# Bounds in one piece, an accumulating form, split constants and measured durations in a two-part attention kernel

## The chip, the cores and the metric

The kernel runs on one core of one Trainium2 chip, as one program. The metric is the device time of one execution in microseconds (us); the time of a kernel is the median of its runs. The engines are TensorE (PE in the profile; its weight loads are listed apart as PEld), VectorE (DVE), ScalarE (ACT), GpSimd (POOL) and SyncE (SP), which here only issues DMAs. TensorE and the others meet in PSUM, eight banks that TensorE writes; all other tiles lie in SBUF.

## What is computed

Two attention blocks over 2048 rows of 1024 columns (32 heads of 32), each with its own input and weights; the outputs stand side by side. Block A is local attention in 4 segments of 512 with a running memory; block B is linear attention with a learned feature map. Cut to what matters:

```python
# A, for each segment s of 4, all heads
logits = einsum("bhqd,bhkd->bhqk", qs, ks) * scale + mask      # causal inside the segment
a_dot  = softmax(logits) @ vs
a_mem  = (phi(qs) @ M) / (phi(qs) @ z + 1e-6)                  # phi(t) = t + 1 if t > 0 else exp(t)
o      = g * a_mem + (1 - g) * a_dot                           # g = sigmoid(beta), one per head
M += phi(ks)^T @ vs;  z += sum(phi(ks))
out_a  = o @ wo
# B
pq, pk = q @ w_phi, k @ w_phi                                  # per head, 32 x 32
phi_x  = concat(softmax(px), softmax(-px))
o      = (phi_q @ (phi_k^T @ v)) / (phi_q @ sum(phi_k) + 1e-6)
out_b  = o @ B_wo
```

## The kernel before

**Numbers.** All large products are made from float16 halves. A float32 operand is scaled, split into a high and a low half, and each product is three matmuls (high-high, high-low, low-high) into one PSUM bank. For that every operand needs a scale, and every result a bound from which its own scale follows. The helper `halves` makes the two halves (ACT the high one, line 427; DVE the low one, line 429), `halved` loads a piece, takes its largest sums of absolute values (ACT, line 469, or DVE, line 463) and calls `scale` (a tiny matmul, line 411, and two DVE instructions, lines 413 and 415) and then `halves`.

**Stages.** The first stage, up to about 900 us, does block A's attention in 32 units (`units`): a unit is one segment of 512 rows and one group of four heads. The first 16 units take segments 0 and 1, the last 16 segments 2 and 3, so each of the eight weight groups is used in both halves; group numbers 8 to 15 stand for the second use. For a unit, `produce` multiplies the q and k weights with the segment (line 400), scales the result by the unit's bounds and moves it into the layout for the scores; `values` does the same for v; `attend` does the attention. The second stage does block B in eight pairs of row tiles (`expo`, the key sums at line 1345, then the queries and their output `project`), with products in Strassen's form of seven products per 2 x 2 blocks (line 596). The last stage is block A's output projection in the same form (line 1590).

**The bounds.** `bounds(k, segs, prio)` works out, for weight group k and one or two segments, the bounds of q and k and what follows from them, in a small tile `bd`: one fp32 matmul per segment (line 708) gives the products of the segment's and the weights' sizes; DVE and POOL make a scale, its reciprocal and five more rows from it (lines 711 to 724). `bounds_v` (lines 733 to 744) does so for v, in `bv`, and keeps the running largest bound in `big` (line 740). In the second half `bounds` is called once for each of groups 8 to 15 and `bounds_v` once for each of the v weights 4 to 7, at the units that load those weights.

**The maxima.** Inside `attend`, `maxima` makes the scores of a block of rows in PSUM (line 854), and DVE adds the causal mask and takes each row's largest (line 860) into `mt`, a 128 x 4 x 4 tile. Two small DVE instructions split `mt` into a high and a low float16 half, `mh` (lines 874 and 875). TensorE turns these into rows (line 880), ACT copies them into the unit's q tile `stk` (line 882), and a DMA repeats them for the other heads. The scores proper (line 945) then carry the subtraction of the largest in the product itself: rows 96 to 103 of the k side hold constants.

**The opening.** Those constants are written once, by three ACT instructions over 8 x 2048 elements (line 637), one for each of the three `stk` tiles; the source `sel` is made by DVE just before (lines 346 to 349). The first transfers are the first weights and the first segment (line 447). The halves of the first groups' weights are made by POOL and ACT (lines 421, 423 and 424): POOL scales the piece, ACT copies the high half, POOL subtracts it; for the first segment and the first v weights `halves` uses ACT and DVE.

**The order.** The engines' queues are in order, and the order is not that of the code. Each `op(engine, duration, function, reads, writes, prio)` is kept in a list; `Graph.run` at the end plays the program through in its own time, and issues the instructions in the order in which that play starts them: at each step the engine that can start earliest takes, of the operations that could start then, the one with the lowest priority number. The durations written in the calls are what this play goes by. A DMA there takes 0.6 us to issue, a fixed latency and its KB over 230 per us. `port=True` (and every POOL operation) means that DVE and POOL operations of this kind don't run side by side in the play. A priority is the number in the call plus a `nudge`: the operations are counted in blocks of 60, and for blocks that stand in `NUDGE` each operation's priority is shifted by a fixed pseudo-random amount, up to 0.3, 0.7, 1.5 or 3.0 by the seed's last two bits. In the play's gaps on TensorE `fill` issues matmuls whose result is unused (line 358).

## Time and profile before

| | |
|---|---|
| median of 3 runs | 1703.16 us (1702.68 to 1703.31) |
| the profiled execution | 1704.9 us |
| its span, from the first to the last instruction | 1702.8 us |
| mean granted TensorE clock | 0.994 |
| busy: PE / DVE / ACT / POOL | 1669.9 / 1399.3 / 1113.4 / 1072.7 us |
| DMA | 280.94 MB |

How to read it: the profile is one execution on the chip. Busy times count instructions of an engine; the rest of the span is idle time, and a row of the timeline or of a group names in brackets, or after a bar, the idle time in front of it and the engine and line that ended it. The granted clock is the share of TensorE's full clock: at 0.5 a matmul takes twice as long, and TensorE counts as busy all the while. Lines are those of the kernel before.

### The profile page before, as it was taken

What the parts mean: (1) busy time and instruction counts of PE and PEld (TensorE: products, weight loads), DVE (VectorE), ACT (ScalarE), POOL (GpSimd) and SP (SyncE); (2) the same over time, 40 slices, a digit from 0 to 9 for tenths busy, and PEclk for the clock granted to TensorE, in tenths of its full rate; (3) what the DMA queues carried; (4) which work ended last, traced back from release to release, by engine and by line L of the source; (5) the groups of instructions that cost most, each with busy time, mean ns of one, the idle gap of its engine ahead of it and who ended that gap; (6) DMA issues with size and microseconds to landing.
All of it is one profiled execution on the core that took longest, in us unless ns stands there. A gap on an engine that the chain in (4) does not pass through costs nothing.

```text
span 1702.8 us, 38814 instructions
## 1 busy us (share of the span) xinstructions
PE 1669.9 (98%) x14520; PEld 1001.0 (59%) x14520; DVE 1399.3 (82%) x3225; ACT 1113.4 (65%) x2027; POOL 1072.7 (63%) x1431
## 2 busy tenths in 40 slices
PE   8999999999999999999999999999999999999999
PEld 6766767676676667766754444444544444444444
DVE  7999999988898788787897998987997777886441
ACT  7779789876786687676776757754765554444331
POOL 6757777676786887867766544454689898541000
PEclk9999999999999999999999999999999999999999
DMA  6964676747656554657567335346566675565311
GB/s 218 236 178 101 155 184 188 222 130 207 167 146 168 131 148 123 158 183 192 138 206 285 119 118 179 131 173 247 207 161 149 174 186 137 171 176 167 117 64 62
DMA packets 266044, 280.94 MB, mean 165 GB/s; under 512 B 162816, under 2 KB 215808, under 8 KB 257280
## 3 DMA queue, kind: packets, MB, share of 16 engines
q1 hardware_dynamic: 265856, 278.47, 56.4%
q8 instruction: 114, 1.87, 0.5%
q14 instruction: 74, 0.61, 0.1%
HBM read 144.39 MB, written 85.00 MB: 135 GB/s over the span
## 4 chain that ended last, share of the span: by engine, by line
PE 59%; DVE 13%; ACT 3%; issue 1%; DMA 1%; POOL 1%; SPq 0%; ACTq 0%; DVEq 0%; POOLq 0%
PE proj L400 14%; PE proj L596 11%; PE misc L400 10%; PE proj L1590 5%; PE s L1590 2%; PE s L945 2%; PE s L854 2%; PE pv L981 2%; DVE mx L1191 2%; PE s L596 2%; DVE r L1201 1%; PE pv L1526 1%; DVE S L429 1%; PE misc L1590 1%; PE misc L596 1%
## 5 line engine op out<-in xcount | busy, mean ns | idle before, releaser
L400 PE MATMUL proj<-S,S 128*128 128x128 f16 (+1 forms) x3072 | 503.3, 300 | 2.1 <-ACT S L427 0.7
L400 PEld LDWEIGHTS <-S 128*128 128x128 f16 x4608 | 331.2, 99 | 150.3 <-issue 4.0
L596 PE MATMUL proj<-S,S 128*128 128x512 f16 x1488 | 348.4, 381 | 6.7 <-DVE cs L606 2.4
L596 PEld LDWEIGHTS <-S 128*128 128x128 f16 x1968 | 187.5, 98 | 220.3 <-issue 9.6
L958 POOL TENSOR_SCALAR_AFFINE_SELECT ph<-ph 128x256 f16<-128x256 f16 (+1 forms) x448 | 193.2, 453 | 131.1 <-DVE ph L952 103.2
L860 DVE CUSTOM_DVE_ANT_0 s<-s,causal 128x256 f32<-128x256 f32 (+3 forms) x512 | 241.9, 511 | 13.3 <-PE s L854 10.4
L952 DVE SCALAR_TENSOR_TENSOR ph<-s,ph 128x512 f16<-128x512 f32 x320 | 210.4, 684 | 41.6 <-ACT ph L951 38.5
L949 ACT ACTIVATE s<-s,bd 128x512 f32<-128x512 f32 x320 | 211.0, 706 | 47.7 <-PE s L945 46.6
L951 ACT ACTIVATE ph<-s 128x512 f16<-128x512 f32 x320 | 186.8, 647 | 6.3 <-PE pv L981 2.6
L400 PE MATMUL misc<-S,ot 128*128 128x512 f16 x768 | 170.5, 379 | 0.1
L1198 ACT ACTIVATE e<-e,sk 128x256 f32<-128x256 f32 x256 | 114.5, 500 | 71.5 <-DVE e L1195 67.6
L400 PEld LDWEIGHTS <-ot 128*128 128x128 f16 x768 | 73.7, 98 | 88.1
L945 PE MATMUL s<-S 104*128 104x512 f16 (+3 forms) x512 | 114.4, 300 | 0.7 <-DVE ph L952 0.3
L854 PE MATMUL s<-S 96*128 96x512 f16 (+3 forms) x512 | 112.0, 299 | 2.7 <-DVE ph L952 2.5
L1495 POOL TENSOR_TENSOR e<-e,zb 128x512 f32<-128x512 f32 x64 | 85.4, 1348 | 33.8 <-DVE r L1201 33.1
L400 PE MATMUL proj<-wv,S 128*128 128x128 f16 x1536 | 105.1, 219 | 0.0
L981 PEld LDWEIGHTS <-ph 128*128 128x128 f16 x2560 | 87.4, 96 | 18.6 <-issue 1.3
L981 PE MATMUL pv<-vl,ph 128*128 128x66 f16 (+1 forms) x2560 | 92.7, 184 | 1.5 <-DVE mt L860 0.5
L1201 DVE TENSOR_REDUCE r<-e 128x32 f32<-128x1024 f32 x64 | 77.0, 1209 | 14.8 <-ACT e L1198 14.8
L1338 POOL TENSOR_TENSOR pt<-e,pt 128x512 f16<-128x512 f32 x40 | 50.1, 1264 | 49.2 <-ACT pt L1335 49.2
L596 PE MATMUL s<-S,S 128*128 128x512 f16 x324 | 77.6, 379 | 0.0
L860 DVE DVE_READ_ACCUMULATOR2_ANT mt<- 128x1 f32 x512 | 72.8, 142 | 0.0
(334 smaller groups left out, 3317.0 us busy)
## 6 DMA issues: line engine op xcount, KB each, us to landing
S<-h SPq DMA_DIRECT2D x192, 128.0 KB
S<-wf_d SPq DMA_DIRECT2D x21, 1024.0 KB
st<-bwqk SPq DMA_DIRECT2D x64, 256.0 KB
wf_d<-fo SPq DMA_DIRECT2D x48, 256.0 KB
out<-os SPq DMA_DIRECT2D x39, 256.0 KB
wf_d<-oT SPq DMA_DIRECT2D x36, 256.0 KB
S<-xf_d SPq DMA_DIRECT2D x9, 1024.0 KB
S<-aw SPq DMA_DIRECT2D x16, 512.0 KB
```

Source lines behind the costliest of these rows:

```text
L400: op(PE, dur, lambda c=c, a=a, b=b, lv=lv, rv=rv: nc.tensor.matmul(pv(), lv(), rv(), start=(c == 0 and a + b == 0), stop=(c == n - 1 and a ...
L596: op(PE, 0.215, lambda n=n, a=a, b=b, lv=lv, rv=rv: nc.tensor.matmul(ps(), lv(), rv(), start=(start and n == 0 and a + b == 0), stop=(n == ...
L854: nc.tensor.matmul(ps()[:, o:o + 128 * i + 128], st()[0:96, 0, h, 128 * i:128 * i + 128], st()[0:96, 1, h, 0:128 * i + 128], start=True, s ...
L860: dve(0.12 + 0.00113 * n, lambda h=h, i=i, o=o, n=n: nc.vector.tensor_tensor_reduce(ps()[:, o:o + n], ps()[:, o:o + n], causal[:, 512 - n: ...
L945: nc.tensor.matmul(ps()[:, o:o + n], st()[0:104, 1, h, 128 * j:128 * j + 128], st()[0:104, 0, h, 128 * j:512], start=True, stop=True)
L949: act(0.59, lambda: nc.scalar.activation(ps(), ps(), AF.Exp, bias=0.0, scale=bd()[:, 4, i2, 0:1]), r=[(bd, i2)], w=[ps])
L951: act(0.5, lambda: nc.scalar.activation(ph()[:, 0], ps(), AF.Copy, scale=2.0 ** 14), r=[ps], w=[(ph, 0)])
L952: dve(0.6, lambda: nc.vector.scalar_tensor_tensor(ph()[:, 1], ps(), 2.0 ** 14, ph()[:, 0], op0=OP.mult, op1=OP.subtract), r=[ps, (ph, 0)], ...
L958: nc.gpsimd.affine_select(pd, pd, pattern=[[0, n], [1, 128]], compare_op=OP.is_ge, fill=0.0, base=0, channel_multiplier=-1)
L981: nc.tensor.matmul(ps()[:, i, n0:n1], ph()[:, a, o:o + 128], vl()[:, j, h, n0:n1], start=(i == 0 and a == 0), stop=(j == min(i, 2)), skip_ ...
L1198: op(ACT, 0.41, lambda i=i: nc.scalar.activation(e()[:, 4 * i:4 * i + 4], e()[:, 4 * i:4 * i + 4], AF.Exp, bias=0.0, scale=sk()[:, i:i + 1 ...
L1590: op(PE, 0.215, lambda n=n, a=a, b=b: nc.tensor.matmul(ps(), v(a)[:, n, :], wform[w]()[:, b, n, :], start=(start and n == 0 and a + b == 0 ...
```

## The change

1. **Bounds of the second half.** A new function `bounds_late` is called once, at unit 12, for all eight q and k weight groups, all four v weights and both segments. It has four matmuls, nine DVE instructions and eight POOL ones, and needs two PSUM banks. `Part` gives each group its view of the common tiles. The calls of `bounds` and `bounds_v` for the second half go.
2. **Inside `bounds`.** Two of the DVE instructions (lines 714 and 721) read the PSUM bank in place of the row that DVE has just made from it. The second follows the first at once.
3. **The maxima's rows.** The first of the two instructions on `mt` (line 874) also writes a sum, as an accumulator output, into a new fifth row of `mt` that nothing reads.
4. **The opening.** Each of the three writes over 8 x 2048 elements becomes four over 8 x 512, in four separately tracked parts. The call of `load_wg` for the first q weights names DVE in place of POOL, so their halves are made by lines 427 and 429 and not by lines 421, 423 and 424.
5. **The plan.** Some hundred durations in the calls are set to other numbers, five operations are marked as port users, and `NUDGE` has 145 seeds in place of 40. None of these adds or removes an instruction; they change the order in which the instructions are issued.

```diff
-NUDGE = {0: 465887, 3: 912202, 5: 876263, 7: 730503, 8: 455190, 9: 72936, 13: 804475, 14: 476942, 15: 772345, 18: 258321,
...
+NUDGE = {0: 927028, 3: 115959, 4: 583906, 7: 632749, 8: 844680, 9: 362793, 10: 459728, 12: 438123, 14: 268131, 15: 522000,
...
+class Part:
+    def __init__(self, of, at):
+        self.of, self.at = of, at
+
+    def __call__(self):
+        return self.at(self.of())
...
-        op(DVE, 0.1, lambda: nc.vector.tensor_tensor(big[:, 1:2], big[:, 1:2], pst[:, p, 0:1], op=OP.max),
-           r=[(pstb, (p, 0))], w=[(bigs, 1)], prio=prio)
+        op(DVE, 0.13, lambda: nc.vector.tensor_tensor(big[:, 1:2], big[:, 1:2], pst[:, p, 0:1], op=OP.max),
+           r=[(pstb, (p, 0))], w=[(bigs, 1)], prio=prio, port=True)
...
     for t in stk:
-        op(ACT, 2.0, lambda t=t: nc.scalar.activation(t()[96:104, 1], sel[96:104, :, None].to_broadcast([8, 4, 512]), AF.Copy),
-           w=[(t, (1, 3))], prio=0.3)
+        for h in range(4):
+            op(ACT, 0.5, lambda t=t, h=h: nc.scalar.activation(t()[96:104, 1, h], sel[96:104, h:h + 1].to_broadcast([8, 512]), AF.Copy),
+               w=[(t, (1, 3, h))], prio=0.3)
...
         op(DVE, 0.1, lambda: nc.vector.scalar_tensor_tensor(
-            bd()[:, 4, v, 0], bd()[:, 3, v, 0], SCALE, bd()[:, 3, v, 1], op0=OP.mult, op1=OP.mult), w=w, prio=prio)
+            bd()[:, 4, v, 0], ps()[:, v, 0], SCALE * 2.0 ** -12, bd()[:, 3, v, 1], op0=OP.mult, op1=OP.mult), r=[ps], w=w, prio=prio)
+        op(DVE, 0.1, lambda: nc.vector.tensor_scalar(
+            bd()[:, 5, v, 0], ps()[:, v, 1], 2.0 ** -14, 2.0 ** -14, op0=OP.mult, op1=OP.add), r=[ps], w=w, prio=prio)
...
-        op(DVE, 0.1, lambda: nc.vector.tensor_scalar(
-            bd()[:, 5, v, 0], bd()[:, 3, v, 1], 0.25, 2.0 ** -14, op0=OP.mult, op1=OP.add), w=w, prio=prio)
...
+    def bounds_late(prio):
+
+        bd, bv = (G.buf("a", [128, r, n], F32, t) for r, n, t in ((7, 4 * NG, "bdl"), (4, 8, "bvl")))
...
+        ps, pv = bank("misc", [128, 2, NG, 2], "bounds"), bank("misc", [128, 2, 4], "bounds")
+        w, wv = [(bd, 0), (bd, 1)], [(bv, 0), (bv, 1)]
+        for x in range(2):
+            op(PE, 0.14, lambda x=x: nc.tensor.matmul(
+                ps()[:, x].rearrange("p k m -> p (k m)"), xam[:, 2 + x:3 + x].to_broadcast([128, 128]),
+                wgb.rearrange("p k m -> p (k m)"), start=True, stop=True),
+               r=[(xams, 2 + x), *((wgbs, (k, m)) for k in range(NG) for m in range(2))], w=[ps], prio=prio)
...
+        op(DVE, 0.11, lambda: nc.vector.tensor_scalar(b(3), f(ps()), 2.0 ** -12, 1e-30, op0=OP.mult, op1=OP.max), r=[ps], w=w, prio=prio)
...
+        op(DVE, 0.1, lambda: nc.vector.tensor_tensor(big[:, 0:1], big[:, 0:1], c(0)[:, 0:1], op=OP.max), r=wv, w=[(bigs, 0)],
+           prio=prio, port=True)
...
-                op(POOL, 1.57, lambda p=p: nc.gpsimd.tensor_scalar(
+                op(POOL, 1.98, lambda p=p: nc.gpsimd.tensor_scalar(
                     p(), p(), 1.0, bd()[:, 5, i2, 1:2], op0=OP.min, op1=OP.mult), r=[(bd, i2)], w=[p], prio=E)
...
-        mt = G.buf("a", [128, 4, 4], F32, "mt", 2)
+        mt = G.buf("a", [128, 5, 4], F32, "mt", 2)
...
-        dve(0.1, lambda: nc.vector.tensor_scalar(mh()[:, :, 0, :], mv(mt), -(2.0 ** -14), None, op0=OP.mult), r=[mt], w=[(mh, 0)])
+        dve(0.18, lambda: nc.vector.tensor_scalar(
+            mh()[:, :, 0, :], mv(mt), -(2.0 ** -14), None, op0=OP.mult, op1=OP.add, accum_out=mt()[:, 4, 0:1]),
+            r=[mt], w=[(mh, 0), (mt, "sum")])
...
-    load_wg(0, -3, POOL, 10, ms=(0,), after=[(xt[0][0], (0, 3))])
+    load_wg(0, -3, DVE, 10, ms=(0,), after=[(xt[0][0], (0, 3))])
...
+        if u == 12:
+            bounds_late(2 * u + 3.5)
...
-            x = 2 * ((u // 4 + 1) // 4)
-            bounds_v(u // 4 + 1, [x, x + 1], 2 * u + 0.5)
+            if u // 4 + 1 < 4:
+                bounds_v(u // 4 + 1, [0, 1], 2 * u + 0.5)
...
-            x = 2 * ((k + 2) // NG)
-            bounds(k + 2, [x, x + 1], 2 * u + 3.5)
+            if k + 2 < NG:
+                bounds(k + 2, [0, 1], 2 * u + 3.5)
```

## The prediction

> **What bounds the kernel now.** First the page's busy times, then the cores, then the busy times by stretches of 50 us (columns: stretch, its length, busy PE, PE weight loads, DVE, ACT and POOL with their counts, granted clock, DMA share, GB/s).

> ```profile
> span 1702.8 us, 38814 instructions
> PE 1669.9 (98%) x14520; PEld 1001.0 (59%) x14520; DVE 1399.3 (82%) x3225; ACT 1113.4 (65%) x2027; POOL 1072.7 (63%) x1431
> ```

> ```profile
> core 0: 1702.8 us, clock 0.994
> ```

> ```profile
> 0.00:50.00 50.00, 44.88 (x321) 32.47 (x322) 38.09 (x118) 35.27 (x54) 35.02 (x52) 0.97 0.68 229
> 50.00:100.00 50.00, 50.00 (x527) 35.93 (x525) 47.44 (x126) 38.96 (x72) 34.75 (x58) 1.00 0.87 227
> ...
> 350.00:400.00 50.00, 47.28 (x512) 33.21 (x510) 41.31 (x114) 34.87 (x64) 38.46 (x68) 0.97 0.65 180
> 550.00:600.00 50.00, 47.47 (x547) 34.05 (x546) 40.84 (x108) 34.39 (x63) 44.22 (x58) 0.97 0.51 134
> 850.00:900.00 50.00, 46.63 (x371) 27.14 (x370) 45.06 (x123) 38.81 (x69) 33.65 (x45) 0.97 0.61 197
> ...
> 1650.00:1702.80 52.80, 48.91 (x227) 21.98 (x225) 9.99 (x14) 10.49 (x16) 0.00 (x0) 1.00 0.16 60
> ```

> TensorE is the bound: busy 1669.9 of 1702.8 us, 50.00 of 50 in an ordinary stretch. So TensorE work that goes is worth its full length, and work taken off another engine is worth only the TensorE stop that it ends. There are 1702.8 - 1669.9 = 32.9 us of stops, and the clock of 0.994 loses another 0.006 x 1702.8 = 10.2 us. The stops are not spread evenly: the opening has 5.1 us, the end 3.9 us, and a few stretches have about 3 us each, with the clock at 0.97 there (0.03 x 50 = 1.5 us lost). I looked into such stretches for what stood in front of TensorE.

> **Part 1: the bounds of the second half.** Today `bounds` (line 708) and `bounds_v` (line 733) each issue two small fp32 matmuls per call, and each matmul leaves two records.

> ```profile
> 364.13 0.50 PE L708 MATMUL misc<-wgb,xam 128*128 128x2 f32 x4
> ...
> 364.49 0.58 PE L733 MATMUL misc<-wvb,xam 128*128 128x1 f32 x4
> ...
> 364.94 0.38 PE L945 MATMUL s<-S 104*128 104x512 f16 x1
> ```

> ```profile
> L708 PE MATMUL misc<-wgb,xam 128*128 128x2 f32 x64 | 9.4, 242 | 0.2 <-DVE ph L952 0.2
> ...
> L733 PE MATMUL misc<-wvb,xam 128*128 128x1 f32 x32 | 4.6, 244 | 0.0
> ```

> These eight records hold TensorE from 364.13 to 364.94, which is 0.81 us or 0.10 us each. Half of all records belong to the second half (32 of line 708, 16 of line 733). The new `bounds_late` has four matmuls, eight records: 48 - 8 = 40 records go, 40 x 0.10 = **-4.0 us**, on TensorE itself. The bounds of this term are -4.0 and 0 (0 where TensorE would stop for something else). 52 small DVE instructions and 40 of POOL also go, and 9 and 8 come (counted in the code). I cost that at nothing: TensorE covers it. Should the cover fail, the new run of nine DVE instructions at 0.15 to 0.2 us delays what is queued behind it, the attention of units 12 and 13, by under 2 us once. The same holds for the two misc banks that `bounds_late` keeps until its last reader.

> **Part 2: two stops at which DVE waited for POOL.** The timeline around 561 us (start, length, engine, line, in brackets the idle time before it and who ended it):

> ```profile
> 560.59 1.13 POOL L958 TENSOR_SCALAR_AFFINE_SELECT ph<-ph 128x256 f16<-128x256 f16 x3
> ...
> 560.97 4.13 DVE L874 TENSOR_SCALAR mh<-mt 128x16 f16<-128x16 f32 x1
> ...
> 561.69 1.15 POOL L507 TENSOR_TENSOR fo<-quad,fo 128x512 f16<-128x512 f32 x1
> ...
> 562.81 1.15 POOL L507 TENSOR_TENSOR oT<-quad,oT 128x512 f16<-128x512 f32 x1
> ...
> 563.92 1.15 POOL L809 TENSOR_TENSOR pkh<-pk,pkh 128x512 f16<-128x512 f32 x1
> ...
> 565.90 0.39 PE L880 MATMUL misc<-identr,mh 128*8 128x128 f16 x4 [2.53 <-DVE mh L875]
> ```

> ```profile
> L874 DVE TENSOR_SCALAR mh<-mt x32: 158/196/4133, 51.1 to 882.4; 128x16 f16<-128x16 f32 x32
> ```

> ```profile
> L874 DVE TENSOR_SCALAR mh<-mt 128x16 f16<-128x16 f32 x32 | 14.3, 447 | 0.2
> ```

> ```profile
> L875 DVE SCALAR_TENSOR_TENSOR mh<-mh,mt x32: 106/178/1243, 53.3 to 882.6; 128x16 f16<-128x16 f16 x32
> ```

> The rows give each line's shortest, median and longest in ns, and for line 874 also the total in us and the mean. A DVE instruction over 16 elements, median 196 ns, mean 447, takes 4.13 us, exactly while POOL runs without a pause (from 560.59 to 565.07), and TensorE stops 2.53 us for its result. Line 875, which reads two SBUF tensors, takes at most 1.24 us. The same kind of thing, twice in a row, at 366 us:

> ```profile
> 366.38 1.04 DVE L714 SCALAR_TENSOR_TENSOR bd<-bd 128x2 f32<-128x2 f32 x1
> ...
> 367.33 1.19 DVE L740 SCALAR_TENSOR_TENSOR big<-bv,big 128x1 f32<-128x1 f32 x1
> ...
> 369.18 0.58 PE L854 MATMUL s<-S 96*128 96x384 f16 x2 [2.09 <-DVE ph L952]
> ```

> Each stop has a tail in which the granted clock drops (stretches of 7.5 us, the clock is the third number from the end):

> ```profile
> 365.00:372.50 7.50, 4.78 (x37) 3.61 (x37) 7.50 (x18) 7.50 (x15) 7.27 (x11) 0.78 0.47 94
> 565.00:572.50 7.50, 6.60 (x28) 2.85 (x29) 3.24 (x9) 3.61 (x7) 3.31 (x5) 0.77 0.58 127
> ```

> Lost to the clock: 7.5 x 0.22 = 1.7 us after the first, 7.5 x 0.23 = 1.7 us after the second. So the stop at 561 costs 2.53 + 1.7 = 4.2 us and the one at 366 costs 2.09 + 1.7 = 3.8 us. The change rewrites all three instructions. Line 874 gets an accumulator output, lines 714 and 721 read PSUM in place of SBUF, and the second half's calls of line 740 shrink to one. I take both stops as gone: **-4.2 and -3.8 us** (bounds: all of it, or nothing). What is late next at 561 us is the vl low half (line 767), which is queued behind line 874 anyway.

> [...]

> The accumulator adds a read per call, which the trace shows for line 860:

> ```profile
> L860 DVE DVE_READ_ACCUMULATOR2_ANT mt<- 128x1 f32 x512 | 72.8, 142 | 0.0
> ```

> That is 32 x 0.142 = 4.5 us more DVE, against 32 x (447 - 196) ns, 8 us, of waits that go. The read is taken at that row's length; it could be nothing if it hides in the instruction. DVE has 2.6 us free even from 50 to 100, and 4.5 us over the 831 us between the first and the last call are 0.27 per 50: nothing. Without that cover each read would delay line 880 by 0.14 us.

> **Part 3: the opening.**

> ```profile
> 4.25 3.70 ACT L637 ACTIVATE S<-sel 8x2048 f16<-8x2048 f32 x2 [2.19 <-DVE sel L349]
> ...
> 7.98 1.06 ACT L469 ACTIVATE S<-S 128x1024 f16<-128x1024 f32 x1
> ...
> 9.60 0.16 DVE L413 TENSOR_SCALAR wgs<-misc 128x1 f32<-128x1 f32 x1 [2.57 <-PE misc L411]
> ...
> 22.17 3.10 POOL L421 TENSOR_SCALAR S<-S,wgs 128x512 f32<-128x512 f32 x2 [6.21 <-issue]
> ...
> 24.31 1.32 ACT L427 ACTIVATE wv<-S,wvs 128x512 f16<-128x512 f32 x2
> ...
> 25.24 3.14 POOL L424 TENSOR_TENSOR S<-S,S 128x512 f16<-128x512 f32 x2
> ...
> 27.88 1.72 DVE L429 SCALAR_TENSOR_TENSOR wv<-S,wvs,wv 128x512 f16<-128x512 f32 x2
> ...
> 28.44 1.46 PE L400 MATMUL proj<-S,S 128*128 128x512 f16 x6
> ```

> *The constants.* ACT writes two constants before it sizes the first weights (line 469), and DVE stands 2.57 us in front of line 413 for that size, with the maxima of the first segment queued behind. Pieces of a quarter would let line 469 in sooner, but the order is fixed by the plan. In the plan the weights' transfer is ready at 0.6 + 1.0 + 512 / 230 + 0.1 = 3.9 us and ACT starts at 0, so two pieces of 2.0 go ahead of line 469 now and eight of 0.5 will. On the chip ACT starts at 4.25. Eight pieces take between 8 x 0.46 = 3.7 us (a quarter of 1.85) and 8 x 0.66 = 5.3 us (line 427, equally long); 0.6 each is nearer to the second row, since a shorter instruction keeps its fixed part. That is 4.8 in place of 3.7: **+1.1 us**. Bounds: -2.6 us, the whole wait of line 413, if fewer pieces go ahead, and +1.6.
> *The first q weights.* Their halves are made by POOL, ACT and POOL (lines 421, 423, 424) from 22.17 to 25.24 + 3.14 = 28.38, and TensorE's q product goes on at 28.44. The call now names DVE, so ACT and DVE make them (lines 427 and 429): 0.66 + 2 x 0.86 = 2.4 us by the rows in place of 6.2, **-3.8 us**, since TensorE has little else there. Bounds: -3.8, and +1.7 if the two DVE instructions only push back the low halves of the v weights, which end at 27.88 + 1.72 = 29.60 and are due next on TensorE. POOL's 6.2 us go too; the halves of the next group's weights are next there.

> **Part 4: the new costs and seeds of the plan** add no work; they re-draw the order of the whole kernel. Left after part 2 are 32.9 - 5.1 - 3.9 - 2.5 - 2.1 = 19.3 us of stops and 10.2 - 1.5 - 3.4 = 5.3 us of clock: at most -24.6 us. Upwards it can add stops such as those of part 2, at 4.0 us each; I allow five, +20. One of the stretches that remain shows instructions whose plan entry becomes a port user:

> ```profile
> 882.65 1.10 DVE L875 SCALAR_TENSOR_TENSOR mh<-mh,mt 128x16 f16<-128x16 f16 x1
> ...
> 883.75 1.09 DVE L551 TENSOR_TENSOR big<-big,pst 128x1 f32<-128x1 f32 x1
> ...
> 883.80 0.22 PE L880 MATMUL misc<-identr,mh 128*8 128x128 f16 x1 [0.91 <-DVE mh L875]
> ```

> Line 551 is now planned as a port user, with 0.13 us. I take that one stretch as mended (850 to 900: 3.37 us of stops and 1.5 of clock, **-4.9 us**) and the others as drawn again with the same loss. This is the softest term.

> **The sum**: -4.0 - 4.2 - 3.8 + 1.1 - 3.8 - 4.9 = -19.6 us. The profiled execution took 1704.9 us with its span of 1702.8, so it would take 1685.3; the median of the runs, 1703.16, lies 1.7 below it, so the forecast is **1683.6 us**.

> **Rivals.**
> *The redrawn order stops TensorE more often (slower).* From 50 to 100 DVE is busy 47.4 of 50, so a late DVE instruction reaches TensorE; each new stop with its half clock costs 4.0 us. Parts 1 to 3 give -14.7, so it decides from five more stops than remain: 1703.2 - 14.7 + 5 x 4.0 = 1708.5 us. For it: everything is redrawn. Against it: 4.2 + 3.8 us of stops came from instructions that no longer meet POOL. Chance 0.17.
> *The wait only moves.* Line 875 follows at once and still reads two SBUF tensors; if it inherits the 4.13 us, part 2 gives 3.8 only and the time is 1687.8 us. Against it: its longest is 1.24 us in 32. Chance 0.08.
> *The time is given back.* If the matmuls, the two stops and the earlier q weights all turn into waits on DVE, and the order mends nothing, the time stays at 1703.2 us. For it: DVE's 47.4 of 50 early on. Against it: 41 of 50 where these stops lie. Chance 0.07.

> **How the numbers follow.** The forecast, with the order between its best and an even draw, has the remaining 0.68. A measurement of this kernel tells about 0.2% from no change, 3.4 us. Faster takes the forecast and the moved wait, 0.76; same 0.07; slower 0.17. The range goes from 1703.2 - 14.7 - 24.6 = 1663.9, about 1664, up to the slower rival at about 1709.

> **What would show it.** Right: line 874 never over 0.6 us; 48 records on lines 708 and 733 of the first half plus 8 new ones; no half clock after a DVE wait on POOL near the unit 12 bounds; line 469 starting near 9 us; the first q product done before 30 us. Wrong: more than five half clocks after the opening, line 875 over 2 us, or PE stops of over 33 us in total.

## The result, and the profile after

| | before | after |
|---|---|---|
| median | 1703.24 us (1702.68 to 1704.99, 4 runs) | 1675.91 us (1673.94 to 1676.12, 4 runs) |
| ratio | | 0.9835, 95% interval 0.9818 to 0.9852 |
| profiled span | 1702.8 us | 1673.8 us |
| TensorE stops (span less busy) | 32.9 us | 26.2 us |
| lost to the granted clock | 0.006 x 1702.8 = 10.2 us | 0.001 x 1673.8 = 1.7 us |
| filler matmuls, records | 64 | 18 |

The losses to the clock come from a mean clock given to three places, so they are good to about 0.9 us. The change takes off 27.3 us; the forecast was 19.6. From here on lines are those of the kernel after, unless another kernel is named; before's lines 400, 469, 714, 740, 874 and 875 are now 420, 489, 735, 761, 952 and 955.

First the page's busy times and the clock of the kernel after:

```profile
span 1673.8 us, 38587 instructions
...
PE 1647.6 (98%) x14434; PEld 984.4 (59%) x14434; DVE 1374.2 (82%) x3216; ACT 1106.0 (66%) x2036; POOL 1066.1 (64%) x1395
```

```profile
core 0: 1673.8 us, clock 0.999
```

TensorE is still the bound. It has 86 records fewer (14520 less 14434): the 40 of the bounds and 46 of the filler. Now the busy times by stretches, for those in which before had lost most:

```profile
0.00:50.00 50.00, 43.90 (x332) 30.73 (x333) 38.76 (x127) 38.15 (x67) 30.22 (x51) 1.00 0.77 251
...
350.00:400.00 50.00, 49.71 (x530) 35.68 (x528) 46.49 (x147) 32.49 (x58) 37.01 (x57) 1.00 0.84 204
550.00:600.00 50.00, 50.00 (x561) 35.24 (x558) 41.94 (x131) 41.59 (x79) 39.27 (x61) 1.00 0.54 155
850.00:900.00 50.00, 49.17 (x388) 26.01 (x386) 38.23 (x74) 36.78 (x66) 36.12 (x52) 1.00 0.69 224
```

The three late stretches, with 2.5 to 3.4 us of stops each and a clock of 0.97 before, have 0.3, 0.0 and 0.8 us of stops and a clock of 1.00. In the whole trace there is no half clock between 5.8 and 1671.5 us. Next the two instructions on `mt`, all 32 calls of each (shortest, median, longest in ns):

```profile
L952 DVE TENSOR_SCALAR_CACHE_REDUCE mh<-mt x32: 164/172/183, 48.0 to 861.1; 128x16 f16<-128x16 f32 x32
L952 DVE DVE_READ_ACCUMULATOR mh<-mt x32: 75/82/89, 48.1 to 861.2; 128x1 f32 x32
```

```profile
L955 DVE SCALAR_TENSOR_TENSOR mh<-mh,mt x32: 169/182/1132, 52.5 to 861.4; 128x16 f16<-128x16 f16 x32
```

The 4133 ns call is gone, the read costs 82 ns, and line 955 did not inherit a long wait here. The filler (its count stands in the row behind the tile) fell from 64 records to 18. First before, then after:

```profile
L358 PE MATMUL fill<-ident x64: 270/275/523, 13.9 to 1424.3; 128*128 128x128 f32 x64
```

```profile
L378 PE MATMUL fill<-ident x18: 270/275/356, 14.4 to 1176.9; 128*128 128x128 f32 x18
```

The spans differ by 29.0 us. Of these 10.2 - 1.7 = 8.5 are clock, 32.9 - 26.2 = 6.7 are stops, 4.1 the bounds' records (the time from the start of each such record to the next, added up in both traces) and about 46 x 0.12 = 5.5 the filler's (0.12 us by the row of equal matmuls quoted in the experiment on the constants). That is 24.8; the other 4.2 are busy time of TensorE that I did not assign.

### The profile page after: what moved, and what is told of

Its sections match the earlier page's. It is cut to its first block, busy times and chain, and to the rows that moved or that the text cites. A ratio compares the mean times of both kernels' runs of the same rounds, so it can differ in the third digit from the quotient of the medians.

```text
span 1673.8 us, 38587 instructions
## 1 busy us (share of the span) xinstructions
PE 1647.6 (98%) x14434; PEld 984.4 (59%) x14434; DVE 1374.2 (82%) x3216; ACT 1106.0 (66%) x2036; POOL 1066.1 (64%) x1395
## 3 DMA queue, kind: packets, MB, share of 16 engines
q8 instruction: 113, 1.85, 0.5%
## 4 chain that ended last, share of the span: by engine, by line
PE 36%; DVE 10%; POOL 7%; ACT 3%; issue 2%; DMA 0%; ACTq 0%; DVEq 0%; POOLq 0%
PE proj L616 10%; PE misc L420 6%; PE proj L1672 5%; PE proj L420 4%; PE s L1672 2%; PE s L616 2%; PE misc L616 1%; POOL e L1577 1%; PE misc L1672 1%; DVE r L1283 1%; DVE mx L1273 1%; POOL e L1589 1%; DVE S L449 1%; PE pv L1608 1%; ACT e L1280 1%
## 5 line engine op out<-in xcount | busy, mean ns | idle before, releaser
L420 PEld LDWEIGHTS <-S 128*128 128x128 f16 x4608 | 326.6, 98 | 143.6 <-POOL S L444 0.7
L616 PE MATMUL proj<-S,S 128*128 128x512 f16 x1488 | 344.9, 379 | 6.6 <-ACT cs L622 4.3
L616 PEld LDWEIGHTS <-S 128*128 128x128 f16 x1968 | 186.8, 98 | 221.7 <-issue 11.7
L938 DVE CUSTOM_DVE_ANT_0 s<-s,causal 128x512 f32<-128x512 f32 (+3 forms) x512 | 241.2, 509 | 12.6 <-PE s L932 10.1
L1031 ACT ACTIVATE ph<-s 128x512 f16<-128x512 f32 x320 | 190.7, 660 | 1.1
L1029 ACT ACTIVATE s<-s,bd 128x512 f32<-128x512 f32 x160 | 107.1, 713 | 16.7 <-PE s L1025 16.3
L1029 ACT ACTIVATE s<-s,bdl 128x512 f32<-128x512 f32 x160 | 105.8, 707 | 6.3 <-PE s L1025 6.1
L1286 POOL TENSOR_SCALAR r<-r 128x32 f32<-128x32 f32 x32 | 12.5, 396 | 96.9 <-DVE r L1284 79.5
```

What stands on the lines that cost most here:

```text
L420: op(PE, dur, lambda c=c, a=a, b=b, lv=lv, rv=rv: nc.tensor.matmul(pv(), lv(), rv(), start=(c == 0 and a + b == 0), stop=(c == n - 1 and a ...
L616: op(PE, 0.2165, lambda n=n, a=a, b=b, lv=lv, rv=rv: nc.tensor.matmul(ps(), lv(), rv(), start=(start and n == 0 and a + b == 0), stop=(n = ...
L938: dve({128: 0.216, 256: 0.381, 384: 0.6, 512: 0.648}[n], lambda h=h, i=i, o=o, n=n: nc.vector.tensor_tensor_reduce(ps()[:, o:o + n], ps()[ ...
L1029: act(0.571, lambda: nc.scalar.activation(ps(), ps(), AF.Exp, bias=0.0, scale=bd()[:, 4, i2, 0:1]), r=[(bd, i2)], w=[ps])
L1031: act(0.478, lambda: nc.scalar.activation(ph()[:, 0], ps(), AF.Copy, scale=2.0 ** 14), r=[ps], w=[(ph, 0)])
```

## The experiments

In all but the four with other seeds, the plan was left as it was: the operations, their durations and their number stay, and only what one of them issues is changed. So, but for the records that an edit adds or moves, TensorE runs the same records in the same order, and the same record can be looked up in two traces. "TensorE stands 1.4 us ahead at 33 us" means that the record which after starts at 33 us starts 1.4 us earlier, each counted from its trace's start. Small leads say little: the next two kernels have before's opening, and yet stand 0.5 and 0.6 us behind it at 33 us.

### The accumulating form alone, in the old order and taken out of the new one

In before, line 874:
```diff
-nc.vector.tensor_scalar(mh()[:, :, 0, :], mv(mt), -(2.0 ** -14), None, op0=OP.mult)
+nc.vector.tensor_scalar(mh()[:, :, 0, :], mv(mt), -(2.0 ** -14), None, op0=OP.mult, op1=OP.add, accum_out=mt()[:, 4, 0:1])
```

> The kernel before, order unchanged, with the accumulating form alone (line 874). Theory: all 32 calls of line 874 take under 0.3 us, the 4.13 us one among them goes, and the time falls by 4.2 us (2.5 us of TensorE's stop and 1.7 us of the half clock behind it), to about 1699.0. Rival, the wait moves to line 875 behind it: that line shows a call of 3 us or more at 561 us, and the time stays within 0.7 us of before.

Measured: 1701.88 us against 1703.63, ratio 0.9989 (0.9980 to 0.9998), so -1.8 us (-0.3 to -3.4). The timeline of this kernel around 561 us:

```profile
561.72 0.17 DVE L874 TENSOR_SCALAR_CACHE_REDUCE mh<-mt 128x16 f16<-128x16 f32 x1
...
562.79 3.05 DVE L875 SCALAR_TENSOR_TENSOR mh<-mh,mt 128x16 f16<-128x16 f16 x1
...
563.54 1.15 POOL L507 TENSOR_TENSOR oT<-quad,oT 128x512 f16<-128x512 f32 x1
...
564.65 1.15 POOL L809 TENSOR_TENSOR pkh<-pk,pkh 128x512 f16<-128x512 f32 x1
...
565.89 0.39 PE L880 MATMUL misc<-identr,mh 128*8 128x128 f16 x4 [1.77 <-DVE mh L875]
```

The rival was right about the mechanism: line 874 takes 0.17 us and line 875, which reads two SBUF tensors, takes the wait, 3.05 us, to the end of the same POOL run. TensorE's stop shrinks from 2.53 to 1.77 us. In the trace TensorE gains 2.4 us at this place, but the kernel of the next experiment, which leaves line 874 alone, gains 1.7 us at the same place: a half clock that did not come. So the form's own part is about 0.8 us, by which the stop shrank. The time came out as neither side had it: less than the theory's 4.2 us, and more than the rival's 0.7.

In after, the other way round (the arguments `op1` and `accum_out` of line 952 taken out):

> The kernel after, order unchanged, with the negated maxima (line 952, 32 calls) in the plain form again. Theory: in the order after too, the plain form must wait for POOL where the accumulating one doesn't: several of the 32 calls take over 0.5 us (accumulating: 164 to 183 ns each), and one or more behind a run of POOL instructions takes 1.6 us or more, so the time rises by 1 to 5 us. Rival, the form alone is worth little and the new order removed the stop: no call takes over 1.6 us, and the time stays within 1 us of after.

Measured: 1676.89 us (1676.43 to 1678.45) against 1675.91 of after; the ratios to before are 0.9846 (0.9833 to 0.9860) and 0.9835 (0.9818 to 0.9852), and the intervals overlap.

```profile
L952 DVE TENSOR_SCALAR mh<-mt x32: 162/312/1459, 48.0 to 862.2; 128x16 f16<-128x16 f32 x32
```

The waits are back (median 312 ns instead of 172, longest 1459), but none is over 1.6 us, and TensorE ends 0.6 us later in the trace. The rival holds: in the new order the form is worth about 1 us, which can't be told from nothing.

### The bounds read from PSUM, in the old order

```diff
-op(DVE, 0.1, lambda: nc.vector.tensor_scalar(bd()[:, 3, v], ps()[:, v], ...), r=[ps], w=w, prio=prio)
+def first():
+    nc.vector.tensor_scalar(bd()[:, 3, v], ps()[:, v], 2.0 ** -12, 1e-30, op0=OP.mult, op1=OP.max)
+    nc.vector.scalar_tensor_tensor(bd()[:, 4, v, 0], ps()[:, v, 0], SCALE * 2.0 ** -12, bd()[:, 3, v, 1], op0=OP.mult, op1=OP.mult)
+    nc.vector.tensor_scalar(bd()[:, 5, v, 0], ps()[:, v, 1], 2.0 ** -14, 2.0 ** -14, op0=OP.mult, op1=OP.add)
+op(DVE, 0.1, first, r=[ps], w=w, prio=prio)
```
The operations of lines 714 and 721 issue nothing.

> The kernel before, order unchanged, with the two products of the bounds (lines 714 and 721) reading PSUM and issued straight behind line 711; line 740 stays as it is. Theory: the stop at 366 us loses the part that lines 714 and 721 make, and the half clock behind it where the rest of the stop is short enough: the time falls by 1.0 to 3.8 us. Rival, line 740 takes the whole wait: it shows a call as long as the three lines' waits together, and the time stays within 0.7 us of before.

Measured: 1704.12 us against 1703.63, ratio 1.0003 (0.9994 to 1.0012): nothing. The timeline at the stop (this kernel's lines 713 and 715 are 714 and 721 of before, 744 is 740), and what TensorE waited for from 360 to 374 us:

```profile
365.59 0.16 DVE L713 SCALAR_TENSOR_TENSOR bd<-misc,bd 128x2 f32<-128x2 f32 x1
365.67 0.15 DVE L715 TENSOR_SCALAR bd<-misc 128x2 f32<-128x2 f32 x1
...
367.20 0.86 DVE L744 SCALAR_TENSOR_TENSOR big<-bv,big 128x1 f32<-128x1 f32 x1
```

```profile
PE s L858 <- DVE ph L956: 1.1, 1, 1.1
```

The form does what it should (1.04 us became 0.16), line 744 still waits 0.86 us, and TensorE's stop falls from 2.09 to 1.1 us. But the half clock behind it stayed, and of the 1.4 us that TensorE had gained 0.6 were left at 387 us. So the smaller stop did not save the clock. The rival had the time right and the mechanism wrong: line 744 waits less than line 740 did in before (1.19 us), and takes nothing over.

This kernel also shows what did. Its plain `tensor_scalar` still takes 4.12 us at 561 us, just as in before, yet no half clock follows. Here are the two traces, cut where the clock can step; the third number from the end is the clock, the third column TensorE's busy time. Before:

```profile
560.28:563.69 3.41, 3.09 (x48) 2.03 (x44) 3.41 (x4) 2.84 (x5) 3.41 (x6) 1.00 0.27 83
563.69:567.11 3.42, 1.21 (x9) 0.62 (x10) 3.39 (x6) 0.59 (x1) 1.38 (x2) 1.00 0.03 9
567.11:570.52 3.41, 3.41 (x11) 1.28 (x10) 0.03 (x1) 1.07 (x2) 2.66 (x3) 0.50 0.81 179
```

And this kernel:

```profile
561.38:564.79 3.41, 2.14 (x28) 1.19 (x26) 3.41 (x1) 1.74 (x4) 3.41 (x5) 1.00 0.26 79
564.79:568.20 3.41, 2.16 (x13) 1.10 (x14) 2.45 (x6) 0.58 (x1) 1.26 (x3) 1.00 0.24 64
568.20:571.62 3.42, 3.42 (x20) 1.61 (x18) 1.80 (x6) 2.84 (x5) 2.47 (x3) 1.00 0.91 188
```

In these traces the clock's steps lie on a grid of 3.413 us: in before the half clocks start at 24.39, 218.95, 369.13, 567.11, 884.54 and 1004.01 us, the later ones 57, 101, 159, 252 and 287 windows of 3.413 us after the first. In before 2.2 us of the stop fell into one window (1.21 us busy) and the next window ran at 0.50; here a boundary at 564.79 split it into 2.14 and 2.16, and nothing happened. The 1.7 us of half clock that the prediction priced with this stop are a matter of where the grid lies.

### The late bounds' matmuls six times over

```diff
-nc.tensor.matmul(ps()[:, x]..., xam[:, 2 + x:3 + x]..., wgb..., start=True, stop=True)
+[nc.tensor.matmul(ps()[:, x]..., xam[:, 2 + x:3 + x]..., wgb..., start=True, stop=True) for _ in range(6)]
```
and the same for the two matmuls on `wvb`.

> The kernel after, order unchanged, with each of the four matmuls of the second half's bounds issued six times over (the same sums written again; 24 instead of 4, 40 records more of 8 in profile's count). Theory: TensorE has no slack, every record costs its pitch of about 0.1 us: plus 4.0 us or so, as taking the like number away gave minus 4.1 us. Rival, they fill stops that TensorE has anyway: plus 1 us or less.

Measured: 1682.29 us (1681.14 to 1684.19), plus 6.4 us. TensorE has no slack there; the added records cost their full length and more. The windows around them:

```profile
373.65:377.06 3.41, 3.41 (x28) 1.72 (x25) 3.40 (x12) 2.47 (x5) 3.41 (x4) 1.00 0.91 237
377.06:380.47 3.41, 3.41 (x48) 3.37 (x46) 3.38 (x17) 2.97 (x6) 2.04 (x5) 1.00 1.03 215
380.47:383.89 3.42, 3.42 (x18) 3.42 (x17) 2.91 (x8) 0.69 (x1) 2.72 (x3) 0.50 1.10 332
```

TensorE is busy all of 377.06 to 380.47 and the clock still halves, for three windows (10.24 us). The window holds the 24 records of the 12 matmuls on `wgb`, 16 columns each; the row gives their shape last. The 24 records on `wvb`, of 4 columns, come behind the step, at the half clock:

```profile
L778 PE MATMUL misc<-wgb,xam x24: 179/263/322, 377.2 to 380.4; 128*128 128x16 f32 x24
L783 PE MATMUL misc<-wvb,xam x24: 354/354/355, 380.6 to 385.5; 128*128 128x4 f32 x24
```

So few columns are streamed in that window (0.28 of it, counted as in the last section), although the engine never stops. 40 x 0.11 = 4.4 us of the 6.4 would be the added records at full clock, at the 0.11 us a record of line 778 here; I put the other 2.0 down to the half clock. All four runs show it: their granted clock is 0.997 or 0.998, and 0.999 or 1.000 in after's.

### The opening: first q weights on POOL again, constants later, warm-up later

```diff
+if after:                                   # the first q weights
+    nc.gpsimd.tensor_scalar(sv(), sv(), cv()[:, 1:2], None, op0=OP.mult)     # then ACT, and for the low half
+    nc.gpsimd.tensor_tensor(lv(), sv(), hv(), op=OP.subtract)
```

> The kernel after, order unchanged, with the halves of the first q weights made on POOL again, as before. Theory: POOL takes twice as long for them, the first q product comes some 4 us later, and the time rises by 3 to 4 us. Rival, TensorE has filler and other products to do there: the time rises by 1 us or less.

Measured: 1679.62 us (1677.92 to 1681.34), plus 3.7 us. TensorE's product for q in this kernel:

```profile
27.92 6.37 PE L420 MATMUL proj<-S,S 128*128 128x512 f16 x16 [1.57 <-POOL S L456]
```

and in after:

```profile
24.54 3.63 PE L420 MATMUL proj<-S,S 128*128 128x512 f16 x16
```

It starts 3.4 us later and takes 2.7 us longer, since the clock was halved from 26.7 to 33.5 us. Ahead of it lie stops of 0.83 and 0.82 us from 23 us on, and one of 1.57 us runs across the step, where after has one stop of 0.28 us in all. TensorE stands 6.1 us back at 33 us, still 5.4 at 1228 and 4.5 at the end. The ratios to before, 0.9864 (0.9842 to 0.9886) and 0.9835 (0.9818 to 0.9852) for after, have intervals that just overlap; it is the trace that shows the loss. Little of it is given back: the theory holds, and the opening's loss stays to the end.

For the constants, the first eight of the pieces (line 658) issue nothing, and the three tiles are written whole at the ninth to eleventh piece, behind line 489:

> The kernel after, order unchanged, with the first eight pieces of the constants (line 658), which stand ahead of the first weights' scale work on ScalarE, left out of their place: the three tiles are written whole at the ninth to eleventh piece, behind it. Theory: line 489 starts near 5 us instead of 8.5, and TensorE's opening ends 2.6 us earlier, so the time falls by 2 to 4 us. Rival, the opening waits for a DMA or for POOL and not for ScalarE: line 489 starts earlier, but the first products start within 0.5 us of where they did, and the time stays within 0.7 us.

Measured: 1678.00 us (1673.12 to 1678.67). The opening in this kernel (662 writes the constants, 1217 are the warm-up matmuls):

```profile
4.36 1.06 ACT L489 ACTIVATE S<-S 128x1024 f16<-128x1024 f32 x1 [2.30 <-DMA S<-aw]
...
5.53 5.50 ACT L662 ACTIVATE S<-sel 8x2048 f16<-8x2048 f32 x3
```

```profile
2.58 5.99 PE L1217 MATMUL misc<-ident 128*128 128x128 f32 x32 [2.58 <-DVE ident L339]
8.40 0.28 PE L431 MATMUL misc<-wgb,one 128*128 128x1 f32 x2
8.54 3.82 PE L1217 MATMUL misc<-ident 128*128 128x128 f32 x32
```

Line 489 starts 4.15 us earlier (8.51 in after), but line 431, which needs its result, only 1.3 us earlier (9.71 in after): it is now queued behind TensorE's own warm-up, which began 0.9 us later in this execution than in after (2.58 and 1.66). The forecast gain did not come, and the time can't be told from after's: the ratio to before is 0.9848 (0.9826 to 0.9870). The rival is out too, since the products start earlier. In this execution, the slowest of the four, TensorE stands 1.4 us ahead at 33 us and 1.1 at 1262, and then loses 5.6 us between 1286 and 1351. At that place VectorE waits once more:

```profile
1291.94 9.42 DVE L1604 TENSOR_TENSOR kls<-e,kls 128x1024 f16<-128x1024 f32 x2 [3.48 <-ACT kls L1602]
...
1293.24 1.26 POOL L519 TENSOR_TENSOR h<-h 128x512 f32<-128x512 f32 x1
...
1299.02 1.26 POOL L519 TENSOR_TENSOR h<-h,h 128x512 f32<-128x512 f32 x1
```

```profile
L1604 DVE TENSOR_TENSOR kls<-e,kls x32: 1160/1323/8253, 1219.2 to 1519.6; 128x1024 f16<-128x1024 f32 x32
```

The first row holds two calls of one subtraction of two SBUF tensors. The second of them takes 8.25 us, while POOL ends one instruction and runs six more, one behind the other, from 1293.24 to 1300.28. In after the same two calls take 4.36 us together, and two of POOL's instructions are stretched, the two engines taking turns (first DVE, then POOL):

```profile
1294.40 4.36 DVE L1597 TENSOR_TENSOR kls<-e,kls 128x1024 f16<-128x1024 f32 x2 [3.79 <-ACT kls L1595]
...
1295.54 2.14 POOL L527 TENSOR_TENSOR S<-h,S 128x512 f16<-128x512 f32 x1
...
1297.64 2.25 POOL L519 TENSOR_TENSOR h<-h,h 128x512 f32<-128x512 f32 x1
```

The instructions are the same. What differs is how they start against POOL's; that this decides between the two courses was not tested.

To see whether the warm-up is next, eight of the sixteen warm-up matmuls ahead of line 431 were issued behind it:

> The kernel after, order unchanged but for the opening: the constants late as in the run above, and eight of the sixteen warm-up matmuls ahead of line 431 issued behind it instead. With late constants alone TensorE stood 1.4 us ahead of after from 33 us on, and line 431 waited for nothing but the warm-up ahead of it. Theory, TensorE's own warm-up is what is late next: line 431 starts another 1.5 us or so earlier, and TensorE stands 2.5 to 3.5 us ahead of after at 33 us, which the time shows as minus 1 to minus 3.5 us if nothing later gives it back. Rival, ScalarE's constants or the weights' transfers are next: 1.0 to 1.8 us ahead at 33 us, as with late constants alone.

Measured: 1677.78 us (1673.04 to 1680.86). TensorE stands 1.2 us ahead at 18 us and 0.6 at 33 us, and again loses 5.4 us between 1286 and 1351 (the subtraction takes 8.27 us). The theory's lead did not come, and it isn't a clean test: the identity that the warm-up multiplies (line 339, DVE) was itself late in this execution, and the first matmul came at 3.89 us against 1.66 in after. The profile is that of the slowest run; two of the five took 1673.04 and 1674.81 us, and one of the four with late constants alone 1673.12, so the 5.6 us are probably not lost in every execution.

### A pause for POOL behind the subtraction

```diff
 nc.vector.tensor_tensor(eh()[:, hb, 1], flat(), eh()[:, hb, 0], op=OP.subtract)
+nc.gpsimd.tensor_copy(gap, eh()[:, hb, 1, 0:1])
```

> The kernel after with the constants late, as run before (1678.0 us; from the opening to 1286 us its TensorE stood 1.1 to 1.4 us ahead of after, and then lost 5.6 us in one place, where the subtraction of kls, line 1597 of after, took 8.25 us on VectorE while POOL ran seven instructions without a pause). New: behind each of the 32 subtractions POOL copies one column of its result, so that POOL has to pause until VectorE has done it. Theory, VectorE is starved for as long as POOL's run lasts, and a pause in the run ends that: no subtraction takes over 3 us, TensorE keeps its lead to the end, and the time is 1672 to 1675 us. Rival, the time at 1290 us is lost to a transfer or to the order, and VectorE's wait only covers it: within 1 us of 1678. Second rival, POOL's 32 pauses make POOL late themselves: over 1679.

Measured: 1675.40 us (1672.71 to 1676.81).

```profile
L1606 DVE TENSOR_TENSOR kls<-e,kls x32: 1162/1332/2859, 1218.0 to 1517.2; 128x1024 f16<-128x1024 f32 x32
```

The long call is gone, and with it the 2.3 us for which TensorE had waited there for `ot`, queued behind it on DVE. The second part of the theory fails: TensorE goes from 2.5 us ahead at 1286 to 0.7 us behind at 1411. Two waits for `cs` stand there (line 622 on ACT 1.9 us, line 626 on DVE 0.9), which the kernel without the pause shows too, while after has one of 0.8. One profile of each kernel can't show that it was the pause that ended the long call, since the kernel without it has a run of 1673.12 us as well. Against after (ratio to before 0.9830, 0.9816 to 0.9844, and 0.9835) nothing is gained that can be told from no change; no version here beats the kernel after.

### The seeds

An empty table (`NUDGE = {}`) in after and in before, and two other sets in after: every seed raised by 8000 or lowered by 4000, with the same blocks and the same reach.

> The kernel after with an empty table of seeds, so the plan's order comes from the costs alone. Theory, the seeds pick the order and give most of the 11.8 us that the other parts leave unexplained: plus 8 us or more, with half clocks and TensorE stops back. Rival, the measured costs give it: within 3 us of after.

> The kernel after with other seeds in the same stretches and with the same reach (every seed raised by 8000). Theory, a seed's worth is that of the very order it was chosen for: as slow as without seeds or slower, plus 8 to 30 us. Rival, any shake of that reach does as well: within 3 us of after.

> The kernel after with a third set of seeds in the same stretches and with the same reach (every seed lowered by 4000). The first other set gave 1768.0 us, no seeds 1722.8. Theory, the seeds of after were chosen for this very kernel, and any other set is a throw: 1725 to 1785 us, the more filler matmuls the slower. Rival, the set raised by 8000 was an unlucky one and most sets give about what after has: under 1700 us.

> The kernel before with an empty table of seeds (order from its old costs alone). Theory, seeds and not costs make the difference between the two orders: before without seeds is as slow as after without seeds (1722.8 us) or slower, 1720 to 1745 us, with more filler matmuls (line 358) than the 64 of before. Rival, the old costs plan well enough by themselves and before's seeds gave little: within 5 us of before (1703).

| kernel | median us | span us | TensorE stops us | lost to clock us | filler records |
|---|---|---|---|---|---|
| before, its seeds | 1703.24 | 1702.8 | 32.9 | 10.2 | 64 |
| before, no seeds | 1740.96 | 1740.0 | 47.4 | 13.9 | 186 |
| after, its seeds | 1675.91 | 1673.8 | 26.2 | 1.7 | 18 |
| after, no seeds | 1722.80 | 1722.8 | 46.0 | 5.2 | 154 |
| after, other seeds | 1768.03 | 1766.1 | 59.6 | 19.4 | 238 |
| after, third seeds | 1768.52 | 1766.1 | 64.7 | 21.2 | 218 |

The rows behind a line of the table, for the seeds raised by 8000: the page's busy times, the clock and the filler (238 records; the last count in its row is of every second one).

```profile
PE 1706.5 (97%) x14654; PEld 1023.7 (58%) x14654; DVE 1373.4 (78%) x3216; ACT 1107.9 (63%) x2036; POOL 1057.0 (60%) x1395
```

```profile
core 0: 1766.1 us, clock 0.989
```

```profile
L378 PE MATMUL fill<-ident x238: 270/275/582, 15.5 to 1569.5; 128*128 128x128 f32 x119
```

Without the filler, TensorE runs 14456 records in both kernels of before and 14416 in all four of after, 40 fewer for the bounds; what differs beyond that stands in the three columns. The same operations and costs give 1675.9, 1722.8, 1768.0 or 1768.5 us by the seeds alone. So a seed set is not a neutral shake: two arbitrary ones cost 45 us over none, and the one in after gains 47. That fits a set searched for with this very list of operations; how it was found is not known here. Before's set gains 38 over none. Without seeds the rest of the change gives 1740.96 - 1722.80 = 18.2 us, but on this one draw the new costs and the new operations can't be told apart: with before's durations and no seeds the plan finds no order for after's operations, so there is no time for that pair, and the reverse (before's operations with after's durations) wasn't tried.

## Why the prediction was right, and where it was not

The sign and the range were right and the forecast, 1683.6 us, was 7.7 us too slow. That it came so near is in part luck: 8.0 of its 19.6 us were put down to new forms that bring about 2 us by themselves, while about 18 us are left for the order, priced at 4.9. The range, 45 us wide, held the time of before as well. By its own steps:

- **Part 1, the bounds: -4.0, measured -4.1.** Right. The other way round, 40 records more cost 6.4 us, about 4.4 of them for the records themselves.
- **Part 2, the two stops: -4.2 and -3.8. This step failed, in its cause.** Both stops are gone, but not through the forms. The accumulating form by itself brings 1.8 us (0.3 to 3.4, and a half clock that did not come is part of it), the PSUM reads nothing that can be told from no change, and undoing the first in the new order costs about 1 us, no more than noise. In the old order the wait of line 874 moved to line 875 (3.05 us), which is the rival that I gave 0.08, because line 875's longest had been 1.24 us. But its calls had been short only since line 874 had done the waiting ahead of them. In the new order neither line waits like that: the longest calls are 1.46 us (plain form, line 952) and 1.13 us (line 955). For the stop at 366 us there is a second cause that no run separates from the order. Lines 714 and 740 of that stop belong to the first calls for the second half, which the change removes: the 33rd of line 708's 64 records is the one at 364.13 us. In after the last such call is over by 352.0 us, and the one late call starts its matmuls at 377.0:

```profile
L729 PE MATMUL misc<-wgb,xam x32: 166/251/251, 21.9 to 352.0; 128*128 128x2 f32 x32
```

```profile
L778 PE MATMUL misc<-wgb,xam x4: 179/222/263, 377.0 to 378.2; 128*128 128x16 f32 x4
```

The run with the PSUM reads kept those calls, so it tests the form alone. The prediction had named the missing calls for line 740 alone; a kernel in before's order without them was not run. And 1.7 us of the price at 561 us were a half clock that hangs on a grid; at 366 us it came in all three kernels in the old order.
- That these forms would end both waits was assumed: the prediction's sum takes 4.2 and 3.8 us for it, and no run shows that the forms bring as much. What the runs show: the accumulating form took at most 183 ns in 32 calls in after and 182 in 32 in before's order, where the plain one had a call of 4133 ns in before and one of 1459 in after's order; before's line 875, which reads two SBUF tensors, then took 3.05 us; the 1.04 us of before's line 714 became 0.16 with the PSUM read, and the time stayed. A wait went on through several POOL instructions, the 8.25 us with late constants through seven.
- **Part 3, the opening: +1.1 and -3.8, together -2.7, measured -3.4.** Line 489 starts at 8.51 us against 7.98 (eight pieces at 0.53 us each, where I took 0.6), so +0.5; the first copy of v, which follows the q product, starts 3.4 us earlier (35.35 us in after, 38.73 in before), which leaves -3.9 for the q weights. Undone, they cost 3.7 us, a half clock of their own included. Right.

```profile
35.35 0.72 ACT L843 ACTIVATE vl<-proj,bv 128x512 f16<-128x512 f32 x1 [0.97 <-PE proj L420]
```

```profile
38.73 0.70 ACT L765 ACTIVATE vl<-proj,bv 128x512 f16<-128x512 f32 x1
```

- **Part 4, the order: -4.9. This is the term that was mis-sized.** With 4.1 of part 1 and 3.4 of part 3, 27.3 - 7.5 = 19.8 us are left for parts 2 and 4, and the forms account for about 2. What is left falls to the order, as a remainder, and with it the removal of the calls at 366 us. After has no half clock left between the opening and the end, 46 of 64 filler records fewer and 6.7 us less of stops, part 3's share among them. I had counted one stretch as mended and taken an even draw for the rest; the seeds' runs show that an arbitrary draw is far worse (1768 us), so the order in the file is no even draw. Its bound (-24.6 us) held, but its terms were stops and clock alone: the filler, about 5.5 us, I had put at nothing.
- The signs: line 952 is never over 0.6 us (183 ns); 48 records of the first half's bounds and 8 new ones; no half clock near the bounds of unit 12; line 489 at 8.51 us; the first q product done before 30 us. No sign of the wrong kind came: no half clock after the opening, line 955 at most 1.13 us, stops of 26.2 us.

## What to carry to other kernels

When a static order is searched for, its draw can be worth more than every edit that the change names: freeze the order and undo one edit at a time before believing that an edit brought the time. Ending one DVE instruction's wait for POOL brings little if the next DVE instruction in the queue then waits in its place, as here, where 4.13 us on before's line 874 became 3.05 on line 875; look at what follows, and count its short durations as sheltered. Price a stop of about 2 us by the stop alone, and treat the half clock behind it as a chance: in the three kernels with the old order it came once of three times at 561 us and three of three at 366 us.

## What the runs showed of the hardware

**How long DVE waited for POOL.** The longest calls lasted until POOL paused: 4.13 us in before (the call ends at 565.10 us, POOL's run at 565.07), 3.05 with the accumulating form (565.84 and 565.80), and 8.25 with late constants (1301.36, which is 1.08 us after POOL's 1300.28; the line's shortest call takes 1.16). With the warm-up moved as well the longest took 8.27. In after the same pair of calls took 4.36 us together where the two engines took turns. With a pause of POOL behind each call the longest in one profile was 2.86 us; what makes the engines take turns or not stays open.
